# Turning and copying q and k of two early quads apart, in a squared-ReLU attention with a mixture of adapters, and a new order of work

## The chip, the cores and the metric

The kernel runs on one core of one Trainium2 chip. The core has a matrix engine (PE; PEld is its weight load), a vector engine (DVE), an activation engine (ACT), a general engine (POOL) and an engine for synchronisation and transfers (SP). The metric is the time of one execution in microseconds on the device. Median before: 184.39 us of 4 runs, from 184.19 to 185.39.

## The reference

Two stages follow each other. The first is attention without softmax: 8 batches, 12 heads, sequence 448, head dimension 64. The second takes the attention's output as 3584 rows of 768 and adds the output of two of eight low-rank adapters (rank 16) to each row, weighted by a gate.

```python
def _attn_ref(q, k, v):
    scores = 1.0 / np.sqrt(64) * np.matmul(q, k.transpose(0, 1, 3, 2))
    attn = np.maximum(scores, 0.0) ** 2 / 448
    return np.matmul(attn, v)

def _moe_ref(x, w_gate, A, B):           # x: the attention's output, (3584, 768)
    logits = x @ w_gate                  # 8 experts, the two largest are kept
    # w: softmax over the two kept logits
    # delta = sum over the two experts e of w[e] * (x @ A[e]) @ B[e]
    return x + delta
```

## The kernel before

**Tiling.** Four heads of one batch make a *quad*; there are 3 quads in each of 8 batches, 24 in all. A quad's 448 keys are cut into J = 7 blocks of 64, so the attention is 168 steps n, each a block of keys of one quad against all its 448 queries. Inputs come as float32 and are turned to bf16 by the load itself (`load`, L299: two DMAs of 64 partitions each, issued on POOL).

**A quad's way through the engines.**

- `tp` (L421): PE turns q and k so that the head dimension lies on the partitions. Each turn is 28 small matmuls with the identity (L431), 28 for q (`m`) and 28 for k (`m1`), both into one pair of PSUM banks: q in columns 0 to 447 of each bank, k in 448 to 895, as bf16. One DVE copy of 128x1792 (`ev`, L445) then brings both to the tile `qT`. With `tboth=1` the turns of q wait for the loads of q and of k.
- The first quad is treated apart (L456 to L481). Its k comes in two pieces: three blocks by SP and ACT (`raw`), four by POOL (`k_rest`, L339). The pieces are turned into bank pairs of their own and copied by `piece` (L448, profile line L453); the copy of the k rest is `e2`, 128x512.
- `qk` (L552, matmuls at L565) makes the scores of a step in two banks; at most three steps' scores are held at a time.
- `relu` (L576) scales and clips them to bf16, on ACT (L585) or on DVE (L587); `sq` (L595, L603) squares two or three steps at a time on DVE; `pv` (L610, L629) multiplies by v and sums over a quad's 7 steps.
- `xt_copy` (L647, L658) brings the attention's output to SBUF, turned, as `xt`.

**The second stage.** A table `awg` is made from A and the gate's weights: two loads (L368, L370) and a selector matrix made on POOL (L361, L362), then two fills of 36 pairs of matmuls (`aw_place`, L375; L383), each copied by DVE (L390). For groups of up to three tiles of 128 rows, `gate` multiplies `xt` by `awg` (L675), picks the two largest logits (L696 to L715), scales (`zp`, L719) and turns the result (L736, L745). `outputs` (L777) adds x and the product with B on PE (L790, L795), copies it out of PSUM (L825, L830) and stores it (L846).

**What sets the order.** The program is written out in an order that the kernel itself works out before it is built. `build` makes a list of operations, each with engines that may do it, a duration, the operations that it depends on, and a rank. `schedule` (L122) plays them through on a model: whenever an engine is free, the ready operation of the lowest rank goes (for PE a change of the tiling mode adds `switch`, and a score step goes ahead when ACT would otherwise run dry). Each engine then carries out its operations in that order, strictly, and waits where an input is not there. Three sets of numbers steer this. `C` holds offsets of rank for each kind of operation. `RANKS` adds a quarter of its value to the rank of single operations by their index in the list, and `ENGINES` fixes the engine of some. The landing time of a load comes from `Dma.land` (L111): half a load's time for each of its two DMAs, stretched by 1.3 while the model's DMA clock lies between 4.5 and 13 us, plus 1.5 us, or 2.1 once that clock is past 5. In the plan at most four loads are in flight ("lane").

Index 84 and 86 in the list are the two fills of `awg`, 85 is the copy of the first of them.

Of the kernel before, what the change touches and what calls it, by code (L numbers as in the profile page):

```python
# [14 lines left out]
J = 7  # L15
# [5 lines left out]
S = J * PH  # L21
# [12 lines left out]
def parts(*cuts):  # L34
# [3 lines left out]

C = dict(
    tp_=2.3287, qk_=-3.679, sq_=3.7975, pv_=3.3372, xt_=-1.2131, gate_=-0.65203, id_=-0.78412,  # L40
    out_=-0.80943, zt_=6.6019, a12=(4, 7), late=6, merge_x=0, id2=2.6063, ocap=3, tboth=1, sqs=(2, 2, 3), xback=(15, 23), xblat=1.4, xbdur=1.35, bx=8, xlag=6, xh=2, gl=(2, 1), tqk=-25.0, tqlat=2.0,
    slack=0.12096, switch=5.8257, third=10.0, dve_relu=0.24094, relu_until=400, qk=-2.3217, sq=10,
    pv=1.0506, xt=8.4423, tp=-9.2867, tpe=4.3867, gate_mm=-4.8593, gate=-1.4524, zt=0.2432, zte=2.902,
    id=15.183, out=3.032, pace=6.5353,
)
# [2 lines left out]


RANKS = {  # L50
    0: 9, 125: -15, 128: -31, 133: -17, 144: -3, 165: -18, 170: 51, 171: -5, 174: -25, 177: -13, 179: 16,
    181: -26, 184: -21, 204: 56, 205: 58, 209: 45, 219: -34, 221: 16, 222: 40, 224: -72, 226: -72, 229:
    31, 260: 33, 263: -15, 264: -19, 268: -26, 272: -6, 276: -17, 281: -15, 287: -22, 290: -135, 293:
    -132, 295: -52, 298: -1, 301: -8, 304: -45, 305: -13, 307: -44, 315: -1, 316: -1, 326: 29, 337: 47,
    340: 49, 342: -28, 345: -33, 347: -4, 374: -3, 375: -1, 380: -85, 396: 6, 403: -19, 424: 19, 430: 22,
    432: 12, 448: 88, 451: -48, 453: -40, 490: 2, 495: -21, 496: -4, 500: -13, 503: -15, 507: -16, 510:
    -39, 517: 1, 519: -27, 525: -62, 548: 5, 558: 40, 561: 96, 567: 48, 569: 5, 580: -56, 603: -3, 621:
    -65, 629: -58, 634: -19, 638: -43, 658: -3, 660: -34, 664: 65, 685: 36, 688: 19, 690: -49, 696: -8,
    697: 12, 701: -45, 713: 11, 722: 22, 779: -1, 780: 18, 790: 25, 794: -24, 795: 100, 799: 43, 801: 44,
    804: -68, 805: 13, 806: -37, 807: 86, 823: 5, 824: 23, 828: -53, 830: -65, 838: 10, 844: 7, 866: -83,  # L60
    867: 31, 870: 7, 871: -68, 874: -80, 878: -91, 896: -49, 898: -65, 916: -51, 920: -15, 923: -17, 924:
    -13, 925: -21, 933: 52, 950: 73, 966: 55, 982: -1, 991: -90, 1008: -109, 1021: 35, 1033: 45, 1043:
    -18, 1066: -10,
}
ENGINES = {
    107: "ACT", 109: "ACT", 170: "DVE", 199: "ACT", 215: "DVE", 222: "DVE", 291: "ACT", 373: "DVE", 381:
    "ACT", 402: "ACT", 431: "ACT", 447: "ACT", 457: "DVE", 517: "ACT", 568: "ACT", 573: "ACT", 581:
    "ACT", 677: "DVE", 866: "ACT", 903: "ACT", 981: "ACT", 1036: "ACT",
}

MODE_SWITCH = 0.13
# [11 lines left out]
def dve(n, rate=0.96):  # L83
    return n / (1000.0 * rate) + 0.068
# [20 lines left out]
class Dma:  # L105
# [5 lines left out]
    def land(self, t, o):  # L111
        if o.kind != "load":
            self.free = max(self.free, t - o.dur[o.engs[0]] + 0.6) + o.mb
            return max(self.free + 1.3, t + o.lat)
        if o.engs[0] != "POOL":
            return t + o.lat
        for x in (t - o.dur["POOL"] / 2, t):
            self.free = max(self.free, x + 0.5) + o.mb / 2 * (1.3 if 4.5 < self.free < 13 else 1)
        return self.free + (1.5 if self.free < 5 else 2.1)


def schedule(ops, c=C):  # L122
# [139 lines left out]
def build(k=None, c=C):  # L262


    ops, more, T = [], [], {}
    nc = k.nc if k else None

    def op(*a, to=ops, **kw):
        o = Op(*a, **kw)
        to.append(o)  # L270
        return o
# [18 lines left out]
    PE, DVE, ACT, ANY = ("PE",), ("DVE",), ("ACT",), ("ACT", "DVE")  # L290
# [119 lines left out]
    while n < NS:  # L410
        m = c["sqs"][turn % len(c["sqs"])]
# [7 lines left out]
    loaded, tp_ops, qk_ops, relu_ops, sq_ops, pv_ops, xt_ops = {}, {}, {}, {}, {}, {}, {}  # L419

    def tp(b, q):  # L421


        rank = first_use[b, q] + at("tp", first_use[b, q])
# [56 lines left out]
            return [[e1, *es] + [e2] * (j >= CUT) for j in range(J)]  # L481
        if b >= c["bx"]:
            return turn_qk(b, q)
        m = op(PE, 0.225, lambda: mm(m, 0), deps=[loaded[b, w, q] for w in range(1 + c.get("tboth", 0))], mode="64",
               kind="tp", ni=56, banks=("t", 2), take=("qT",), rank=rank)
        m1 = op(PE, 0.225, lambda: mm(m, 1), deps=[loaded[b, 1, q], m], after=m, mode="64", kind="tp", ni=56,
                give=("k", "q"), rank=rank - 0.5)
        if c.get("tsplit"):
            es = [op(ANY, {"ACT": act(2 * S), "DVE": dve(2 * S, 1.92)}, None, deps=[m1], free=[(m, g)], rank=rank + c["tpe"])
                  for g in range(2)]  # L490
            for g, e in enumerate(es):
                def fn(g=g, e=e):
                    if ("qT", b, q) not in T:
                        new("qT", ("qT", b, q), [128, 2, 2, S], BF16)
                    (nc.scalar.copy if e.eng == "ACT" else nc.vector.tensor_copy)(
                        T["qT", b, q].rearrange("p g w x -> p g (w x)")[:, g], k.ps_b[:, m.banks[g], : 2 * S])
                e.fn = fn
            return [es] * J
        e = op(DVE, dve(4 * S, 1.92), ev, deps=[m1], free=[(m, None)], rank=rank + c["tpe"])
        return [[e]] * J  # L500

# [526 lines left out]
```

## Time and profile before

| | us |
|---|---|
| median of 4 runs | 184.39 |
| the profiled execution | 184.01 |
| its span | 181.9 |
| PE, DVE, ACT, POOL busy | 165.4, 164.5, 155.1, 89.9 |
| granted PE clock, mean over the span | 0.977 |
| end of the last matmul; end of the last copy | 177.4; 178.0 |

The span runs from the first instruction to the last, and the last 3 us or so of it are the stores that land after the last copy. "Busy" counts the time in which an instruction of the engine is under way; neighbours on DVE and ACT can overlap by some tenths of a microsecond. In a row of the timeline, neighbours of one kind are merged: "x4" and a length of 3.35 us are four instructions that end 3.35 us after the first began, and the bracket tells the idle time of the engine before the first and who ended it. PEclk is the matrix engine's granted clock, in tenths of full speed.

### The profile page before, as it was taken

How to read it: one execution, taken by the hardware profiler on the slowest of the kernel's cores; microseconds unless marked ns; L12 is line 12 of the kernel's file. 1: busy time of each engine (PE TensorE's matmuls, PEld its weight loads, DVE VectorE, ACT ScalarE, POOL GpSimd, SP SyncE). 2: the span in 40 equal slices, each digit the busy share in tenths (PEclk: the TensorE clock that was granted, in tenths of full speed). 3: DMA queues.
4: the chain of work that ended last, by engine and by line, in shares of the span. 5: the costliest groups of instructions: out<-in, count | busy, mean ns of one | idle time of the engine just before them, and what ended most of it. 6: DMA issues, size and time to landing. Idle time of an engine off the chain costs nothing.

```text
span 181.9 us, 7406 instructions
## 1 busy us (share of the span) xinstructions
PE 165.4 (91%) x3198; PEld 97.1 (53%) x3198; DVE 164.5 (90%) x258; ACT 155.1 (85%) x226; POOL 89.9 (49%) x155
## 2 busy tenths in 40 slices
PE   7559987869999989999999899999999999999990
PEld 2435854635565556546556466565566456456650
DVE  1568999999999999999999999999999999999941
ACT  3479889999999999999999999999999999961210
POOL 7999789897975979755277636700000000000000
PEclk9956999999999999999999999999999999999998
DMA  5999999999999999999989999999873457555766
GB/s 92 129 159 149 191 188 178 178 169 191 162 199 208 224 227 188 225 193 217 190 129 178 213 223 126 199 134 174 101 123 70 108 130 164 140 140 126 220 178 172
DMA packets 34449, 30.49 MB, mean 168 GB/s; under 512 B 11952, under 2 KB 30896, under 8 KB 34416
## 3 DMA queue, kind: packets, MB, share of 16 engines
q0 software_dynamic: 22000, 17.03, 66.6%
q1 hardware_dynamic: 11792, 11.90, 27.3%
q10 hardware_dynamic: 624, 1.08, 2.3%
q8 instruction: 25, 0.41, 0.9%
q14 instruction: 8, 0.07, 0.2%
HBM read 33.84 MB, written 11.01 MB: 247 GB/s over the span
## 4 chain that ended last, share of the span: by engine, by line
PE 55%; DVE 26%; ACT 11%; issue 4%; DMA 2%; POOL 0%; DVEq 0%; ACTq 0%; POOLq 0%
PE ps L795 19%; PE ps L565 13%; DVE a L603 12%; PE ps L629 11%; ACT a L585 9%; DVE qT L445 6%; PE ps L675 4%; PE ps L790 4%; PE ps L431 3%; DVE xt L658 3%; DVE a L587 2%; DMA q<-in_q_dram 2%; ACT xt L658 1%; PE ps L736 1%; DVE zp L719 1%
## 5 line engine op out<-in xcount | busy, mean ns | idle before, releaser
L585 ACT ACTIVATE a<-ps 128x896 bf16<-128x896 f32 x157 | 136.4, 957 | 5.1 <-PE ps L565 4.8
L603 DVE TENSOR_TENSOR a<-a 128x1792 bf16<-128x1792 bf16 (+1 forms) x72 | 88.2, 1240 | 2.4 <-ACT a L585 2.2
L565 PE MATMUL ps<-qT 64*64 64x448 bf16 x672 | 62.0, 372 | 8.1 <-ACT a L585 4.1
L795 PE MATMUL ps<-B,zT 128*128 128x384 f32 x112 | 47.0, 514 | 0.0
L629 PE MATMUL ps<-a,v 64*64 64x448 bf16 x672 | 44.5, 351 | 1.5 <-DVE qT L445 1.1
L565 PEld LDWEIGHTS <-qT 64*64 64x64 bf16 x672 | 23.9, 107 | 38.0 <-issue 28.0
L307 POOL DMA_DIRECT2D q<-in_q_dram x48 | 29.4, 632 | 16.2 <-PE ps L431 8.5
L307 POOL DMA_DIRECT2D v<-in_v_dram x48 | 29.4, 636 | 6.9 <-PE ps L565 2.6
L307 POOL DMA_DIRECT2D k<-in_k_dram x46 | 28.2, 634 | 3.8 <-DMA q<-in_q_dram 3.1
L629 PEld LDWEIGHTS <-v 64*64 64x64 bf16 x672 | 22.4, 106 | 12.2 <-issue 5.1
L445 DVE COPY qT<-ps 128x1792 bf16<-128x1792 bf16 x23 | 25.0, 1086 | 0.7 <-PE ps L431 0.5
L795 PEld LDWEIGHTS ps<-B,zT 128*128 128x128 f32 x112 | 17.5, 191 | 4.8 <-issue 1.3
L658 ACT CAST xt<-ps 128x448 bf16<-128x448 f32 x25 | 13.9, 585 | 3.4 <-PE ps L629 3.4
L658 DVE CAST xt<-ps 128x448 bf16<-128x448 f32 x23 | 14.0, 617 | 0.3 <-PE ps L629 0.3
L830 ACT COPY osb<-ps 128x384 f32<-128x384 f32 x24 | 12.2, 530 | 1.4 <-PE ps L795 1.4
L587 DVE TENSOR_SCALAR a<-ps 128x896 bf16<-128x896 f32 x11 | 12.0, 1088 | 1.3 <-PE ps L565 1.0
L790 PEld LDWEIGHTS <-xt 128*128 128x128 bf16 x114 | 7.8, 97 | 9.3 <-issue 7.7
L790 PE MATMUL ps<-identb,xt 128*128 128x128 bf16 x114 | 12.7, 221 | 0.0
L431 PEld LDWEIGHTS <-q 64*64 64x64 bf16 x672 | 10.5, 115 | 4.0 <-issue 2.5
L675 PE MATMUL ps<-awg,xt 128*128 128x136 bf16 x168 | 12.5, 223 | 0.0
L675 PEld LDWEIGHTS <-xt 128*128 128x128 bf16 x168 | 10.1, 98 | 3.2 <-issue 3.0
L431 PE MATMUL ps<-identb,q 64*64 64x64 bf16 x672 | 10.5, 199 | 0.6 <-ACT a L585 0.5
(47 smaller groups left out, 96.8 us busy)
## 6 DMA issues: line engine op xcount, KB each, us to landing
out_dram<-osb SPq DMA_DIRECT2D x50, 192.0 KB, 3.5
q<-in_q_dram POOLq DMA_DIRECT2D x48, 112.0 KB, 4.5
v<-in_v_dram POOLq DMA_DIRECT2D x48, 112.0 KB, 5.1
k<-in_k_dram POOLq DMA_DIRECT2D x46, 112.0 KB, 4.9
out_dram<-osb ACTq DMA_DIRECT2D x4, 192.0 KB, 2.7
B<-in_moe_B_dram POOLq DMA_DIRECT2D x1, 384.0 KB, 5.0
xb<-xt SPq DMA_TRANSPOSE x18, 4.0
a_raw<-in_moe_A_dram POOLq DMA_DIRECT2D x1, 192.0 KB, 4.9
```

What stands on the lines that cost most here:

```text
L307: nc.gpsimd.dma_start(out=t[g * PH : g * PH + PH], in_=k.qkv[w][b, g, :, 2 * q : 2 * q + 2, :])
L431: nc.tensor.transpose(k.ps_b[sl * PH : sl * PH + PH, o.banks[g], (w * J + j) * PH : (w * J + j) * PH + PH], source(w, j)[r, sl], k.identb[ ...
L445: nc.vector.tensor_copy(t.rearrange("p g w x -> p g (w x)"), k.ps_b[:, m.banks[0] : m.banks[0] + 2, : 2 * S])
L565: nc.tensor.matmul(out=bank(o, sl)[g * PH : g * PH + PH, at : at + w], lhsT=t[r, g, 1, j * PH : j * PH + PH], rhs=t[r, g, 0, x0:x1], start ...
L585: nc.scalar.activation(out, flat(qk_ops[n], w), ACTF.Relu, scale=k.relu_scale)
L587: nc.vector.tensor_scalar(out, flat(qk_ops[n], w), k.relu_scale, 0.0, op0=ALU.mult, op1=ALU.max)
L603: nc.vector.tensor_mul(a2, T["a1", g0], T["a1", g0])
L629: nc.tensor.matmul(out=bank(head, g)[sl * PH : sl * PH + PH, :w], lhsT=vn[r, sl, j * PH : j * PH + PH], rhs=T["a2", g0][r, i, sl * w : sl ...
L658: evac(w, lambda cp, g=g: cp(k.xt[:, g * QUADS + q, b * S + x0 : b * S + x1], bank(src, g)[:, :w]), deps=[pv_ops[n]], free=[(src, g)], ran ...
L675: nc.tensor.matmul(out=bank(zops[0])[:, t * ZW : t * ZW + ZW], lhsT=k.xt[:, do, 128 * tiles[t] : 128 * tiles[t] + 128], rhs=k.awg[:, do, : ...
L790: nc.tensor.matmul(out=out(h)[:, x * 128 : x * 128 + 128], lhsT=k.xt[:, 3 * h + x, c0 : c0 + 128], rhs=k.identb, start=(x == 0), stop=Fals ...
L795: nc.tensor.matmul(out=out(h)[:, :W], lhsT=T["zT", g0][:, zi], rhs=k.B[:, h * W : h * W + W], start=xb is not None, stop=True, skip_group_ ...
```

## The change

The second and third quads (the quads with index 1 and 2, `apart=3`) no longer turn q only when k has landed too: `m` waits for q alone. A copy `eq` of q (128x896) follows `m`, and a copy `e` of k follows `m1` and `eq`. The score steps of these quads wait for both copies. The other 21 quads and the first are done as before. The bank pair is given back after `e`.

In `Dma.land` the stretch by 1.3 now ends at 8 us instead of 13, and the landing term stays at 1.5 up to 16 us instead of 5. Four planner constants, nearly all of `RANKS` and most of `ENGINES` are new; the arithmetic is the same.

```diff
-... sqs=(2, 2, 3), xback=(15, 23), xblat=1.4, xbdur=1.35, bx=8, xlag=6, xh=2, gl=(2, 1), tqk=-25.0, tqlat=2.0,
-    slack=0.12096, switch=5.8257, third=10.0, dve_relu=0.24094, relu_until=400, qk=-2.3217, sq=10,
+... sqs=(2, 2, 3), xback=(15, 23), xblat=1.4, xbdur=1.35, bx=8, xlag=6, xh=2, apart=3, gl=(2, 1), tqk=-25.0, tqlat=2.0,
+    slack=-0.19633, switch=5.8334, third=4.0894, dve_relu=0.28627, relu_until=400, qk=-2.3217, sq=10,
...
 RANKS = {
-    0: 9, 125: -15, 128: -31, 133: -17, 144: -3, 165: -18, 170: 51, 171: -5, 174: -25, 177: -13, 179: 16,
...
+    0: 5, 84: 115, 85: 162, 86: 87, 132: 10, 141: 53, 148: -11, 150: 39, 155: -32, 156: -8, 157: 13, 158:
+    -9, 160: -12, 163: -20, 166: -25, 170: -15, 179: -51, 185: -11, 191: -5, 192: 35, 200: 50, 210: 36,
...
 ENGINES = {
-    107: "ACT", 109: "ACT", 170: "DVE", 199: "ACT", 215: "DVE", 222: "DVE", 291: "ACT", 373: "DVE", 381:
-    "ACT", 402: "ACT", 431: "ACT", 447: "ACT", 457: "DVE", 517: "ACT", 568: "ACT", 573: "ACT", 581:
-    "ACT", 677: "DVE", 866: "ACT", 903: "ACT", 981: "ACT", 1036: "ACT",
+    140: "ACT", 178: "ACT", 233: "ACT", 265: "ACT", 286: "ACT", 298: "ACT", 568: "ACT", 634: "DVE", 852:
+    "ACT", 866: "ACT", 881: "ACT",
 }
...
-            self.free = max(self.free, x + 0.5) + o.mb / 2 * (1.3 if 4.5 < self.free < 13 else 1)
-        return self.free + (1.5 if self.free < 5 else 2.1)
+            self.free = max(self.free, x + 0.5) + o.mb / 2 * (1.3 if 4.5 < self.free < 8 else 1)
+        return self.free + (1.5 if self.free < 16 else 2.1)
...
-        m = op(PE, 0.225, lambda: mm(m, 0), deps=[loaded[b, w, q] for w in range(1 + c.get("tboth", 0))], mode="64",
+        apart = 3 * b + q < c["apart"]
+        m = op(PE, 0.225, lambda: mm(m, 0), deps=[loaded[b, w, q] for w in range(1 + (not apart))], mode="64",
                kind="tp", ni=56, banks=("t", 2), take=("qT",), rank=rank)
...
+        if apart:
+            eq = op(DVE, dve(2 * S, 1.92), lambda: piece(nc.vector.tensor_copy, m, 0, 0, J), deps=[m], rank=rank + c["tpe"] - 0.5,
+                    to=more)
+            e = op(DVE, dve(2 * S, 1.92), lambda: piece(nc.vector.tensor_copy, m, 1, 0, J), deps=[m1, eq],
+                   free=[(m, None)], rank=rank + c["tpe"])
+            return [[eq, e]] * J
```

## The prediction

> **What bounds the kernel now.** I read the page's busy shares and its 40 slices first (a slice is 4.55 us), then busy time by stretch, then the timeline where those rows show holes.
>
> ```profile
> span 181.9 us, 7406 instructions
> PE 165.4 (91%) x3198; PEld 97.1 (53%) x3198; DVE 164.5 (90%) x258; ACT 155.1 (85%) x226; POOL 89.9 (49%) x155
> PE   7559987869999989999999899999999999999990
> DVE  1568999999999999999999999999999999999941
> ACT  3479889999999999999999999999999999961210
> PEclk9956999999999999999999999999999999999998
> ```
>
> From the fifth slice to about 161 us ACT and DVE are nearly full; from 50 us PE is too. Only the two ends have slack: the last 16 us belong to PE alone (ACT is down to 2 tenths or less from 164 on), the first 24 to nobody. Busy time by stretch (start:end, length, then busy us and instructions in brackets):
>
> ```profile
> 10.50:14.20 3.70, 2.42 (x76) 1.42 (x72) 2.46 (x3) 3.31 (x5) 3.70 (x7) 0.50 1.06 153
> 20.50:24.00 3.50, 3.32 (x114) 2.47 (x112) 3.50 (x6) 2.49 (x4) 3.45 (x6) 1.00 1.09 228
> 24.00:30.00 6.00, 4.36 (x114) 2.48 (x114) 6.00 (x7) 6.00 (x9) 5.50 (x11) 1.00 1.18 175
> 140.00:161.00 21.00, 20.92 (x283) 10.72 (x275) 20.81 (x36) 20.09 (x30) 0.00 (x0) 1.00 0.56 130
> ```
>
> PE works 20.92 of 21.00 us before the tail, but only 4.36 of 6.00 between 24 and 30, where ACT and DVE are full. So work that starts earlier on ACT and DVE can be followed by PE; the end moves if the lead is kept. The timeline (start, length, what; in brackets the idle before it and who ended it) shows what is late:
>
> ```profile
> 7.14 1.09 DVE L587 TENSOR_SCALAR a<-ps 128x896 bf16<-128x896 f32 x1 [0.84 <-PE ps L565]
> 8.34 1.09 DVE L603 TENSOR_TENSOR a<-a 128x1792 bf16<-128x1792 bf16 x1
> 9.35 0.42 DVE L453 COPY qT<-ps 128x512 bf16<-128x512 bf16 x1
> 9.82 1.33 PE L565 MATMUL ps<-qT 64*64 64x448 bf16 x12 [2.40 <-DVE qT L453]
> 10.46 3.35 ACT L585 ACTIVATE a<-ps 128x896 bf16<-128x896 f32 x4 [1.78 <-PE ps L565]
> 11.41 1.09 DVE L603 TENSOR_TENSOR a<-a 128x1792 bf16<-128x1792 bf16 x1 [1.64 <-ACT a L585]
> 12.41 1.08 DVE L445 COPY qT<-ps 128x1792 bf16<-128x1792 bf16 x1
> 14.19 2.54 ACT L585 ACTIVATE a<-ps 128x896 bf16<-128x896 f32 x3 [0.39 <-PE ps L565]
> 21.01 1.73 ACT L585 ACTIVATE a<-ps 128x896 bf16<-128x896 f32 x2 [0.46 <-PE ps L565]
> 23.28 9.93 ACT L585 ACTIVATE a<-ps 128x896 bf16<-128x896 f32 x12 [0.55 <-PE ps L565]
> ```
>
> A copy of 0.42 us stands behind a square of 1.09 us; PE, then ACT, then DVE wait in turn. ACT loses 1.78 + 0.39 + 0.46 + 0.55 = 3.18 us before 24, and not a microsecond more until 50. DVE loses 1.64, and 0.34 and 0.29 later: 2.27.
>
> **The change, part by part.** The order is the planner's, so I ask what its new constants make it believe. By its load rule (issue ends 1.17 us apart on POOL, half a load's time each, plus a landing term), the rest of the first k lands at 7.43 by the old constants and 6.83 by the new; the trace has its second issue at 3.71 and 2.8 to landing: 6.5. The k of the second quad: 10.94, now 10.34; the trace: 6.06 + 3.9 = 9.95. The k of the third: 14.45, now 13.04; the trace: 8.43 + 4.4 = 12.85. All three come nearer.
>
> 1. The copy of 0.42. Its turns ended at 7.41. Believed ready at about 7.3, not 7.85, it stands right after the relu that ends at 8.23 and ahead of the square: done at 8.65 instead of 9.77. ACT took up the next relu 0.69 after the copy (10.46 − 9.77): now at 9.34. ACT's 1.78 shrinks to 9.34 − 8.68 = 0.66. Gain 1.12. The displaced square is late by 0.42, and only PV at 16.83 waits for that chain.
>
> 2. Second quad apart. The turns of q can go at 8.3, when q lands (4.91 + 3.4), and their copy before k lands at 9.95. Then k: some 0.7 of turns at half clock (10.57 to 11.28 for q in this trace), a half copy. No row has a 128x896 copy; between 0.39 for 448 columns and 1.09 for 1792 it is 0.39 + 448 x 0.70/1344 = 0.62. Copied by 11.4, or by 12.5 behind one square of 1.09; ACT could begin the second quad 0.7 later, at 12.1 to 13.2. ACT's own work is there at 9.34 + 3.35 = 12.69. Before it was 14.19: gain 1.0 to 1.5 with step 1 in it; I take 1.4. The third quad's k is there at 12.85, and ACT needs it seven relus (5.9 us) after 12.7: splitting it gains nothing. Two splits cost 2 x (2 x 0.62 − 1.09) = 0.30 on DVE; half of that, 0.15, is felt, as DVE and ACT share work.
>
> Here a rule speaks against the change. The Trainium skill, "PSUM — Partial Sum Buffer", section "PSUM bank collisions raise a hardware error", says two engines must be kept out of one bank and quadrant at the same time, whatever columns they touch. The split q and k share one pair of banks (the first quad's pieces have their own, so no row shows the wait). If the program obeys it, k's turns wait on PE for the q copy on DVE, and all of PE's later work stands behind them. By the columns alone step 2 costs no wait; by the rule it costs nothing if the q copy is done by 9.95, and up to a square, 1.09, if it is queued behind one. That leaves 0.3 of the 1.4 at worst. I take the rule as true and its cost as 0.1: q has 1.65 us ahead of k.
>
> 3. The gate table. Two fills of 36 small matmul pairs stand at 18.84 and 21.30 (1.5 to 1.7 us each); ACT's 0.46 and 0.55 follow them. Ranks +115/4 and +87/4 push both fills back, +162/4 one of their evictions (0.57 each). POOL is reordered too: four loads may be in flight in the plan, and earlier landings free a slot sooner. By hand, the first v passes the two POOL instructions for the selector (0.87 and 0.83), the table's two loads (13.00 to 14.45) fall behind later k, v and q loads to about 18.6. So k of the fourth quad is issued some 1.45 earlier (lands near 19.2, not 20.7), and the table lands at 18.6 + 4.9 = 23.5, not 17.9. SP has nothing here. Gain on ACT: up to 1.01; I take 0.8.
>
> Its price: 3.0 us of PE now lie after 24. PE's idle there is 1.64 up to 30 and 1.50 from 30 to 40, 3.14 together; but a fill in one piece of 1.5 against ACT's 0.87 per relu can starve ACT as it did at 21. I charge 0.8, between 0 (all in the holes) and 1.0 (the two stalls again).
>
> 4. DVE's idle of 2.27 is room for at most two relus (1.09 there, 0.87 off ACT). Between 0 and 1.74 I take 0.4, as the squares also come sooner.
>
> 5. The clock. The Trainium skill, "TensorE: Matmul & The Clock Gate", section "What's actually happening", has PE fall to half speed after an idle window of about 3.4 us. The trace fell with a shorter gap: 2.40 us, and 0.50 granted from 10.5 to 14.2; score matmuls average 517 ns from 4 to 16.8 us, 359 from 30 to 60. By the rule the smaller gap keeps the clock full and may save some 0.3 (an estimate, from 0.69 to about 0.4) at each of two hand-overs; by the trace sparse work keeps it low. ACT sets the pace, so I take 0.
>
> 6. Everything after. Most new ranks lie beyond 50 us, and half the forced engines go. No row shows that order. PE idles 2.15 us between 50 and 161, so at most 2.1 is to be had; were all 111 us as loose as 60 to 80 (0.97 idle in 20) the idle would be 5.4, a loss of 3.2. The nearest row is the present order: 0.
>
> Sum: 1.4 − 0.15 − 0.1 + 0.8 − 0.8 + 0.4 = 1.55, say 1.6. The profiled execution took 184.01 (span 181.9 and 2.1 around it): 182.4. The median, 184.39, lies 0.38 above: **182.8**. A measurement of this kernel can tell about 0.5% (0.92 us) from no change.
>
> **Rivals.** *Carried through* (above): full ACT and DVE from 24, and PE's holes there, speak for it. 0.55; own range 181.5 to 183.6.
>
> *Bank wait*: the split does not start k's turns freely; they wait behind a late q copy once or twice. 1.1 is given back: 183.9. For it: the 1.09 squares on the same engine. Against: q's lead of 1.65. 0.12.
>
> *Absorbed*: the lead turns into more PE idle between 24 and 50, or is lost in the new order, because PE sets the tail. Lead 1.6, minus as much: 184.4. Against it: in the present trace PE follows ACT there at three quarters load. 0.13.
>
> *Slower: the table comes too late.* The gate's first matmuls (L675) stand at 33.6 and the outputs (L795) begin at 46.5. With one eviction pushed by 40 ranks, the gate for the first tiles waits, PE has nothing to fill 34 to 50 with (idle 2.2 already), and the outputs go to the end, where PE is alone: 2.4 us of L795 before 50 and 1.2 of L675, 3.6 in all. 184.4 − 1.6 + 3.6 = 186.4. It decides once more than 2.5 us of them are displaced. For it: the ranks. Against: outputs are 12.8 us of the tail anyway, and the gate runs well before its outputs. 0.20, in which I include a plainly poorer order in step 6.
>
> **How the numbers follow.** Faster: 0.53 of the first, 0.05 of the bank wait, 0.02 of absorbed: 0.60. Same: the rest of those, 0.20. Slower: 0.20. The range takes the low end of the first (181.5) and the slower case up to 186.2, leaving under 0.08 below and 0.12 above.
>
> **What would show it.** Step 1: the 0.42 copy before the square, and ACT's hole at 8.7 under 0.8. Step 2: two half copies near 0.62, the second quad's relus from about 12.7; a PE wait on the q copy would show the bank rule. Step 3: fills after 23.5, no ACT holes near 20 to 23. Carry: at 50 us the same copy of qT about 1.6 earlier, and outputs after 161 still near 12.8 us. The prediction is wrong if PE's idle between 50 and 161 exceeds 2.15 by more than 1, or L795 begins after 50.

## The result, and the profile after

The changed kernel takes 183.75 us (median of 35 runs, 181.71 to 187.25), the kernel before, run beside it, 184.22 (54 runs, 183.36 to 185.39). The ratio of the two is **0.9956, with an interval of 0.9940 to 0.9971**: 0.44% or 0.8 us faster, against 1.6 us predicted. The ratio leaves out runs that are more than 1.5% above the fastest of the same kernel; the changed kernel's fastest run is exceptionally low, so this drops its upper part (8 of 35), and the medians over all runs give 183.75/184.22 = 0.9974. A second set of runs of the same kernel gave 0.998 (0.9958 to 1.0002), and over both sets together (57 runs and 100 beside them) the medians are 183.95 and 184.24. The gain lies between 0.3 and 0.8 us, at the edge of what can be told from no change. The profiled execution is that fastest run of the 35: 181.71 us (span 179.9). Its profile shows the change at its best, and what the other runs lose has to be looked for elsewhere.

The page of the changed kernel, busy shares and the rows of the 40 slices (4.5 us each):

```profile
span 179.9 us, 7410 instructions
PE 163.7 (91%) x3198; PEld 96.6 (54%) x3198; DVE 164.9 (92%) x257; ACT 155.3 (86%) x229; POOL 89.8 (50%) x155
PE   7867698897999999999999999999999999999990
DVE  1599999999999999999999999999999999998860
ACT  3599999999999999999999999999999999951200
PEclk9999999999999999999999999999999999999997
```

DVE and ACT are full from the third slice on, not from the fifth or sixth, and the clock row has lost its 5 and 6. Busy time by stretch of the changed kernel (start:end, length, then PE, PEld, DVE, ACT, POOL with instructions in brackets, granted clock, DMA share, GB/s):

```profile
10.50:14.20 3.70, 2.12 (x80) 1.46 (x81) 3.70 (x5) 3.70 (x6) 3.62 (x7) 1.00 1.06 155
20.50:24.00 3.50, 2.81 (x100) 1.84 (x100) 3.50 (x4) 3.50 (x6) 2.95 (x5) 1.00 1.48 223
24.00:30.00 6.00, 5.62 (x164) 4.21 (x156) 6.00 (x8) 5.95 (x9) 4.77 (x9) 1.00 1.19 195
50.00:161.00 111.00, 109.03 (x2098) 63.80 (x2091) 109.21 (x165) 108.89 (x163) 44.95 (x76) 1.00 0.89 170
140.00:161.00 21.00, 20.76 (x324) 11.40 (x324) 20.59 (x31) 19.45 (x28) 0.00 (x0) 1.00 0.49 113
```

From 10.5 to 24 neither DVE nor ACT idles. PE has 5.62 us of work between 24 and 30 where it had 4.36, because the two fills of the gate table now stand there. Between 50 and 161 PE idles 111.00 − 109.03 = 1.97 us, no more than before (2.15). The timeline of the changed kernel at the start (DVE and ACT rows in order of time):

```profile
7.16 14.85 ACT L591 ACTIVATE a<-ps 128x896 bf16<-128x896 f32 x18 [0.69 <-PE ps L571]
7.38 0.42 DVE L452 COPY qT<-ps 128x512 bf16<-128x512 bf16 x1 [1.08 <-PE ps L430]
7.76 1.09 DVE L593 TENSOR_SCALAR a<-ps 128x896 bf16<-128x896 f32 x1
9.14 0.62 DVE L452 COPY qT<-ps 128x896 bf16<-128x896 bf16 x1 [0.29 <-PE ps L430]
9.69 1.08 DVE L609 TENSOR_TENSOR a<-a 128x1792 bf16<-128x1792 bf16 x1
10.69 0.62 DVE L452 COPY qT<-ps 128x896 bf16<-128x896 bf16 x1
...
13.73 0.61 DVE L452 COPY qT<-ps 128x896 bf16<-128x896 bf16 x1
...
15.73 0.61 DVE L452 COPY qT<-ps 128x896 bf16<-128x896 bf16 x1
...
22.29 2.58 ACT L591 ACTIVATE a<-ps 128x896 bf16<-128x896 f32 x3
```

ACT runs 18 relus in one piece from 7.16 to 22. The copy of 0.42 us stands ahead of the square, ahead even of the first DVE relu, and the half copies of the second and third quad take 0.61 to 0.62. The table's loads are issued at 19.01 and 19.91 (before: 13.00 and 13.90), have landed at 25.2 (before: 18.1), and the fills start at 25.4 (before: 18.84). In the changed kernel:

```profile
19.01 0.91 POOL L367 DMA_DIRECT2D a_raw<-in_moe_A_dram  x1
```

and in the kernel before:

```profile
13.00 0.96 POOL L368 DMA_DIRECT2D a_raw<-in_moe_A_dram  x1
...
18.84 1.68 PEld L383 LDWEIGHTS <-sel 128*128 128x128 bf16 x36 [0.34 <-issue]
```

### Where the lead goes

For the changed kernel and those that keep its order after the start, I took the relus in order of their start, numbered from 0, seven to a quad, and subtracted their starts from those of the kernel before's profile. This "lead" is positive where the run is ahead. Number 21 opens the fourth quad, 63 the tenth, 84 the thirteenth; "last output" is the lead at the end of the last matmul. A load is two transfers, and its landing is that of the later one. The last column but one is a stop of PE that is explained below. *again* is the changed kernel unaltered; the others are described with the experiments.

| profiled execution | second quad's k landed | third quad's q landed | clock 11 to 22 us | lead at 21 | at 63 | at 84 | last output | PE stop near 68 us | span |
|---|---|---|---|---|---|---|---|---|---|
| before | 10.0 | 11.6 | 0.75 | 0 | 0 | 0 | 0 | none | 181.9 |
| after | 10.0 | 11.6 | 1.00 | 3.59 | 2.51 | 1.96 | 2.29 | none | 179.9 |
| again | 10.1 | 12.0 | 0.84 | 2.92 | 1.32 | −0.88 | −0.88 | 1.47 | 183.1 |
| pause | 10.6 | 12.0 | 1.00 | 3.34 | 2.26 | 0.21 | 0.54 | 1.32 | 181.7 |
| room | 10.4 | 12.7 | 0.84 | 3.31 | 2.28 | 0.70 | 0.91 | 0.85 | 181.3 |
| late_a | 12.1 | 12.7 | 0.84 | 1.43 | 0.35 | −0.74 | −0.70 | 0.36 | 182.9 |
| merged | 10.5 | 13.0 | 0.53 | 1.01 | 0.03 | −0.52 | −0.20 | none | 182.4 |

Three things can be read from it. The start lead is 1.0 to 3.6 us, and smallest in the two executions with the latest loads: the second quad's k in *late_a*, the third quad's q in *merged*. From 21 to 63 the order gives back the same 0.98 to 1.08 in five of the six (in *again* 1.60: it had one more stop, 0.48 us at 31.9), and from 63 to 84 another 0.55 where PE doesn't stop. Where PE stops, the loss from 63 to 84 is the 0.55 and the stop and some 0.18 more: 2.20 for 1.47, 2.05 for 1.32, 1.58 for 0.85, 1.09 for 0.36.

### The profile page after: what moved, and what is told of

It is laid out like the page before. It is cut to its first block, busy times and chain, and to the rows that moved or that the text cites. A ratio compares the mean times of both kernels' runs of the same rounds, so it can differ in the third digit from the quotient of the medians.

```text
span 179.9 us, 7410 instructions
## 1 busy us (share of the span) xinstructions
PE 163.7 (91%) x3198; PEld 96.6 (54%) x3198; DVE 164.9 (92%) x257; ACT 155.3 (86%) x229; POOL 89.8 (50%) x155
## 3 DMA queue, kind: packets, MB, share of 16 engines
q1 hardware_dynamic: 11792, 11.90, 25.2%
q10 hardware_dynamic: 624, 1.08, 2.3%
## 4 chain that ended last, share of the span: by engine, by line
PE 57%; ACT 17%; DVE 16%; issue 4%; DMA 2%; POOL 2%; ACTq 0%; DVEq 0%; POOLq 0%
PE ps L801 19%; ACT a L591 14%; PE ps L571 13%; PE ps L635 11%; DVE a L609 8%; PE ps L681 4%; PE ps L796 4%; PE ps L430 2%; DVE qT L444 2%; ACT xt L664 2%; DMA q<-in_q_dram 2%; DVE a L593 2%; PE ps L382 2%; DVE xt L664 2%; DVE qT L452 1%
## 5 line engine op out<-in xcount | busy, mean ns | idle before, releaser
L591 ACT ACTIVATE a<-ps 128x896 bf16<-128x896 f32 x155 | 133.6, 965 | 1.2 <-PE ps L571 0.9
L571 PE MATMUL ps<-qT 64*64 64x448 bf16 x672 | 57.7, 362 | 7.4 <-ACT a L591 5.6
L635 PE MATMUL ps<-a,v 64*64 64x448 bf16 x672 | 43.0, 350 | 1.7 <-ACT a L591 1.6
L571 PEld LDWEIGHTS <-qT 64*64 64x64 bf16 x672 | 22.7, 105 | 35.5 <-issue 27.6
L635 PEld LDWEIGHTS <-v 64*64 64x64 bf16 x672 | 21.7, 106 | 12.0 <-issue 4.6
L444 DVE COPY qT<-ps 128x1792 bf16<-128x1792 bf16 x21 | 22.8, 1084 | 0.1
L664 ACT CAST xt<-ps 128x448 bf16<-128x448 f32 x28 | 15.2, 576 | 3.6 <-PE ps L635 3.6
L593 DVE TENSOR_SCALAR a<-ps 128x896 bf16<-128x896 f32 x13 | 14.1, 1087 | 0.5 <-PE ps L571 0.4
L796 PE MATMUL ps<-identb,xt 128*128 128x128 bf16 x114 | 12.7, 221 | 0.2
L664 DVE CAST xt<-ps 128x448 bf16<-128x448 f32 x20 | 12.2, 618 | 0.7 <-PE ps L635 0.5
L681 PEld LDWEIGHTS <-xt 128*128 128x128 bf16 x168 | 10.4, 98 | 4.4 <-issue 3.9
L430 PEld LDWEIGHTS <-q 64*64 64x64 bf16 x672 | 10.5, 111 | 3.6 <-issue 0.9
L430 PE MATMUL ps<-identb,q 64*64 64x64 bf16 x672 | 10.4, 195 | 0.7 <-DMA q<-in_q_dram 0.3
```

The lines of the kernel that those rows point to most:

```text
L430: nc.tensor.transpose(k.ps_b[sl * PH : sl * PH + PH, o.banks[g], (w * J + j) * PH : (w * J + j) * PH + PH], source(w, j)[r, sl], k.identb[ ...
L444: nc.vector.tensor_copy(t.rearrange("p g w x -> p g (w x)"), k.ps_b[:, m.banks[0] : m.banks[0] + 2, : 2 * S])
L571: nc.tensor.matmul(out=bank(o, sl)[g * PH : g * PH + PH, at : at + w], lhsT=t[r, g, 1, j * PH : j * PH + PH], rhs=t[r, g, 0, x0:x1], start ...
L591: nc.scalar.activation(out, flat(qk_ops[n], w), ACTF.Relu, scale=k.relu_scale)
L593: nc.vector.tensor_scalar(out, flat(qk_ops[n], w), k.relu_scale, 0.0, op0=ALU.mult, op1=ALU.max)
L635: nc.tensor.matmul(out=bank(head, g)[sl * PH : sl * PH + PH, :w], lhsT=vn[r, sl, j * PH : j * PH + PH], rhs=T["a2", g0][r, i, sl * w : sl ...
```

## The experiments

Unless an edit says otherwise nothing of the computation is changed; each kernel is compared with the kernel before, run beside it.

| kernel | what it is | median, us | before | ratio |
|---|---|---|---|---|
| again | changed kernel, unaltered | 184.20 | 184.28 | 0.998 (0.9958 to 1.0002) |
| swap | before, copy of 0.42 ahead of the square | 184.37 | 184.28 | 1.0001 (0.9975 to 1.0028) |
| merged | after, one copy for q and k as before | 183.51 | 184.28 | 0.9951 (0.9927 to 0.9975) |
| latefill | before, three ranks of the table as after | 195.08 | 184.28 | 1.0535 (1.0484 to 1.0586) |
| warm1 | after, 4 zero matmuls at each early score step | 184.61 | 184.23 | 1.0019 (0.9993 to 1.0046) |
| warm2 | after, 8 zero matmuls at fewer steps | 184.49 | 184.23 | 1.0016 (0.9995 to 1.0037) |
| warmb | before, 4 zero matmuls | 188.02 | 184.23 | 1.0201 (1.0164 to 1.0238) |
| swap2 | swap, and the table issued earlier | 183.54 | 184.23 | 0.9966 (0.9943 to 0.9988) |
| late_a | after, second quad's q and all later loads issued some 0.7 later | 184.77 | 184.15 | 1.0017 (0.9996 to 1.0038) |
| late_b | before, second quad's q and all later loads issued some 0.7 later | 184.96 | 184.15 | 1.0049 (1.0029 to 1.0069) |
| room | after, q turned later, third quad in one copy | 183.68 | 184.15 | 0.9969 (0.9942 to 0.9995) |
| pause | after, POOL pauses 3.2 us | 184.35 | 184.25 | 1.0001 (0.9978 to 1.0025) |

### The parts of the start: again, swap, merged, latefill

*again* repeats the changed kernel, to learn how much of the profiled 2.3 us an ordinary execution shows.

> The changed kernel once more, unaltered, for a second profile and the spread of its times. Its first profile (181.71) is the fastest of its 35 executions; their median is 183.75. Theory A, the clock: the executions near 183.5 have lost 1.5 to 2 us in the first 25 us to a PE at half clock; then a profile with a time of 183 or more shows a granted clock near 0.5 somewhere between 8 and 20 us and holes of ACT there of 1 us or more, and over the executions time falls as the mean clock rises. Theory B, loads: PE or DVE wait 1 us or more for a landing at a clock that stays full. Theory C, the middle: the start is as in the first profile, with the fourth quad's first relu near 22.3, and the 2 us go after 50 us.

It measured 0.998, and its profile lies at 184.9, 1.2 us of span longer than before. The same program's two profiled executions differ by 3.2 us; one profile of this order doesn't stand for its median.

*swap* does step 1 alone, in the order of the kernel before:

```diff
+    ops = schedule(build(h))
+    tags = [getattr(o, "tag", None) for o in ops]
+    i, j = tags.index(("sq", 0)), tags.index("rest")
+    ops.insert(j, ops.pop(i))
```

> The kernel before, with one change: in the finished order the copy of the rest of k stands ahead of the first square on DVE instead of behind it. All else keeps its place. Carried through: the copy ends 1.1 us earlier, ACT takes up its fourth relu at about 9.3 instead of 10.5, and the end comes 0.6 to 1.1 us earlier: ratio to the kernel before 0.994 to 0.997. Rival, the order of the rest decides: a start that is 1.1 us earlier is waited away by 50 us, ratio 1.000 within 0.002.

The time is unchanged. The lead is 1.58 at relu 7 and 1.19 at relu 14, and −0.91 at relu 21. Timeline of *swap*: PE's wait, what ACT pays for it, and POOL's issue of the table:

```profile
13.91 0.96 POOL L368 DMA_DIRECT2D a_raw<-in_moe_A_dram  x1
...
20.12 0.22 PE L383 MATMUL ps<-a_raw,sel 128*128 128x128 bf16 x1 [2.39 <-DMA a_raw<-in_moe_A_dram]
...
22.11 1.73 ACT L586 ACTIVATE a<-ps 128x896 bf16<-128x896 f32 x2 [2.76 <-PE ps L566]
```

PE arrives at the first fill, whose place is fixed, 2.39 us before the table has landed; in the kernel before PE got there at 18.84 and the table was there at 18.1, 0.7 us ahead. Step 1 gains what was said, and the next thing late is the table. Of the 2.39, about 0.9 is that execution's own: it issued the table that much later than the kernel before's profile did (13.91 against 13.00).

*merged* keeps the changed order and leaves out the split: the first half copy is gone, and the second copies q and k together.

```diff
-            eq = op(DVE, ..., lambda: piece(nc.vector.tensor_copy, m, 0, 0, J), deps=[m], ...
+            eq = op(DVE, ..., lambda: None, deps=[m], ...
-            e = op(DVE, ..., lambda: piece(nc.vector.tensor_copy, m, 1, 0, J), deps=[m1, eq],
+            e = op(DVE, ..., ev, deps=[m1, eq],
```

> The changed kernel with q and k of the second and third quads copied in one instruction at the place of the second of the two copies; q's own copy is gone, everything else keeps its place. If the split itself brings something: the one copy of 1.09 ends some 0.45 us later than the half copy did, ACT waits for it once, and the time is 0.2 to 0.5 us above the changed kernel's. Rival, the split is worth nothing: ACT has relus to do until then, DVE gets 0.15 us back for each quad, and the time is the changed kernel's within 0.2.

It is as fast as the changed kernel: 0.9951 against 0.9956 and 0.998. What the split brings or costs is below what these runs can tell; the gain is that of the order. Its profile had late loads (the third quad's q at 13.0, against 11.6) and a cold matrix engine, as its busy time by stretch shows:

```profile
11.00:22.00 11.00, 9.34 (x188) 5.44 (x189) 8.98 (x9) 9.38 (x12) 10.72 (x19) 0.53 1.14 162
```

The same stretch of the changed kernel:

```profile
11.00:22.00 11.00, 7.50 (x204) 3.87 (x205) 11.00 (x12) 11.00 (x15) 10.60 (x18) 1.00 1.11 161
```

PE needs 9.34 us at the clock of 0.53 and 7.50 at 1.00, and ACT loses 1.6.

*latefill* moves the table's fills alone: the three ranks of the changed kernel in the kernel before.

```diff
-    0: 9, 125: -15, ...
+    0: 9, 84: 115, 85: 162, 86: 87, 125: -15, ...
```

> The kernel before with three ranks of the changed one: the two fills of the gate table 115/4 and 87/4 later, the copy of the first 162/4 later. The planner plays the order through again, so the rest can move too. Carried through: ACT's two holes of 0.46 and 0.55 near 20.5 and 23 are gone, its relus after 24 are 0.8 to 1.0 earlier, and the end comes 0.3 to 0.8 earlier (ratio 0.996 to 0.998). Rival, the table comes too late: the gate starts later than 33.6, PE has more idle time before 50, and the time is the same or up to 1.5 us longer.

5.4% slower. Waits of *latefill* from 20 to 161 us (engine, line, releaser: us in total, times, longest):

```profile
ACT a L585 <- PE ps L565: 10.1, 16, 1.9
```

ACT is starved 16 times, from 21 to 48 us and again near the end; the lead is −3.4 at relu 42 and −11.1 at 140. The edit did not do what it was meant to: the planner laid out the whole program anew from the three ranks, with all the others still tuned to the old order. It says nothing on step 3, but it does say that searched ranks can't be carried over one by one. All later edits therefore move single operations in the finished order.

### The clock: warm1, warm2, warmb

The half clock of *merged* suggested that the gain is lost where PE runs cold between 10 and 22 us. These kernels put matmuls of zeros into the early score steps, into the bank that the step is about to overwrite, so the result is unaffected.

```diff
+            for sl in range(2 if 3 <= n <= 20 else 0):
...
+                for g in range(2):
+                    nc.tensor.matmul(out=bank(o, sl)[g * PH : g * PH + PH, at : at + w],
+                                     lhsT=k.zeros[r, :PH], rhs=k.zeros[r, :w], start=True, stop=True)
```

> The changed kernel with four more matmuls of zeros ahead of each score step 3 to 20, into the banks that the step then overwrites; they wait for the banks alone, not for q and k, and fill PE's holes between 8 and 22 us. Theory A, the clock: in most executions PE falls to half clock there, and the lead at the fourth quad's first relu shrinks from 3.6 to 1 to 3 us; kept at work PE stays at full clock, the mean granted clock is 0.99 or more in most executions, and the median falls to 182.0 to 183.0 (ratio 0.988 to 0.993). Rival: the clock is a companion, not a cause; the median stays within 0.4 of 183.75, or rises by up to 1 us as the zeros delay the scores.

> As the run with four zeros a step, with eight a step on steps 3 to 16. If activity keeps the clock and four are too few, this one shows the clock at 0.99 or more and the gain of 0.8 to 1.7 us; if the zeros stand in the way of scores, it is 0.3 to 1.5 us slower than with four.

> The kernel before with the same four zeros a step on steps 3 to 20. Its hole of 2.4 us on PE at 7.4 stays, as the bank is the only thing the zeros need. Theory A: its scores of the first quads come at full clock, two hand-overs of some 0.3 us are saved, but its table fill holds the rest back as it waits for the table's landing near 18: 0 to 0.6 us faster. If it gains as much as the changed kernel does (0.8 or more), a warm PE is worth the same to any order and the change's own gain is not limited by it.

All three are slower than what they were made from, the two first by some 0.4 to 0.6%, the kernel before by 2%. Busy time by stretch of *warm2*:

```profile
11.00:22.00 11.00, 9.92 (x302) 6.20 (x290) 9.24 (x11) 9.39 (x12) 10.87 (x18) 1.00 1.13 164
```

and the waits of PE in *warm1* from 30 to 161 us (in its slowest execution, 187.53):

```profile
PE ps L430 <- issue: 3.7, 3, 2.2
```

The clock was full, and no time came of it: with the zeros PE's work in the stretch is 9.92 us, more than *merged* had at half clock, and ACT is no busier (9.39). In *warm1* PE stopped three times besides, 3.7 us together, for nothing that the profile shows ("issue"; taken up below). So the theory that the clock takes the gain isn't supported, but not refuted either: the zeros cost as much PE time as the full clock saves. The sign that was named for it, that time falls as the mean clock rises, did appear in *again*: 183.6 us in the median of the 8 executions with a clock of 0.99 or more, 184.8 in that of the 4 below 0.98. But late loads and a low clock can come together (*late_a* and *merged* in the table), so this doesn't make the clock the cause; and *warm2* had 0.99 or more in 18 of 22 executions and stayed at 184.5.

### Landing times: swap2, late_a, late_b

*swap2* is *swap* with the two table loads issued ahead of the fourth quad's q (one operation moved; the copy and square as in *swap*):

```diff
+    i, j = tags.index("table"), tags.index(("load", 1, 0, 0))
+    ops.insert(j, ops.pop(i))
```

> The kernel before with the copy of the rest of k ahead of the first square, and besides with the table's two loads issued before the fourth quad's q instead of after it. With the copy moved alone, PE waited 2.4 us at the first fill for the table's landing at 20.0 and the lead of 1.6 us was gone. If that wait is the whole reason: the table lands near 18, the wait is under 0.6, and the end comes 0.8 to 1.5 us earlier (ratio 0.992 to 0.996). Rival: the lead is lost in the rest of the order anyway, ratio 0.998 to 1.002.

0.9966, so 0.34% faster than before (0.12% to 0.57%). The table landed at 16.9 and PE no longer waits for it. The profiled execution lost its lead another way, before the table's place, so the evidence is the median. The timeline of *swap2* (POOL's issue, and ACT's hole for the third quad's late loads):

```profile
11.84 0.94 POOL L369 DMA_DIRECT2D a_raw<-in_moe_A_dram  x1
...
19.10 1.88 ACT L587 ACTIVATE a<-ps 128x896 bf16<-128x896 f32 x2 [1.76 <-PE ps L567]
```

Two moved operations give most of what the searched order gives. With *swap* this speaks for it that **the table must leave the way before the first copy is worth anything**, be it earlier or later. The two intervals just overlap, so the times alone don't show it; the wait in *swap* shows the place.

*late_a* and *late_b* delay the second quad's q and k, and with them all later loads, by a fill of zeros on POOL ahead of the load (0.77 us in the profile of *late_a*; the issue comes 0.67 to 0.68 later), in the changed kernel and in the kernel before. The tile that it fills isn't in use yet.

```diff
+            nc.gpsimd.memset(k.sel, 0.0)
```

> The changed kernel with one more fill of the selector on POOL (0.87 us) between the load of k's rest and the load of the second quad's q, so every later load, the table's too, is issued 0.87 us later. Theory B, landings: PE turns the second q at 8.6, and the third at 11.6, as soon as they land, and all of PE stands behind a turn that waits; the shift passes through, 0.5 to 0.9 us slower than the changed kernel (184.2 to 184.7). Rival, loads are no limit: the order has room, 0 to 0.2 slower.

> The kernel before with the same 0.87 us on POOL at the same place. Theory B: its turns stand behind its late copy and waited 0.2 us on loads in all; the second k lands at 10.8 where PE would turn it at 10.9, the third at 13.7 where it is turned at 15, the table at 18.8 where it is used at 18.8: 0 to 0.4 us slower, less than half of what the changed kernel loses. Rival: any order loses the same.

Both lose: the changed kernel goes from 0.9956 or 0.998 to 1.0017, the kernel before to 1.0049, about 0.7 to 1.1 us and 0.9 us. Late loads from the second quad on cost either order about their lateness. My theory that the new order stands tighter on its landings falls: if so, *late_a* would have lost clearly more than *late_b*.

### PE without instructions: room and pause

The stops "for nothing that the profile shows" are also in *again*. Its timeline:

```profile
68.64 0.29 PE L681 MATMUL ps<-awg,xt 128*128 128x136 bf16 x2
...
70.40 0.41 PE L681 MATMUL ps<-awg,xt 128*128 128x136 bf16 x4 [1.47 <-issue]
...
71.18 1.73 ACT L591 ACTIVATE a<-ps 128x896 bf16<-128x896 f32 x2 [1.42 <-PE ps L571]
...
72.13 1.09 DVE L609 TENSOR_TENSOR a<-a 128x1792 bf16<-128x1792 bf16 x1 [1.58 <-ACT a L591]
```

In the middle of one series of gate matmuls, with all operands there, PE does nothing for 1.47 us, and then ACT and DVE wait in turn. Counting PE's weight loads and matmuls from the start of the program, and three other instructions of PE's sequencer among them, every such stop of 0.36 us or more in the fourteen profiles (eleven: two in *again*, three in *warm1*, two in *warmb*, one each in *room*, *late_a*, *late_b*, *pause*) falls on an instruction whose number is 193 more than a multiple of 256; in *again*, *room*, *late_a* and *pause* it is number 2753. The queues of the changed kernel have one row that fits:

```profile
q8 instruction: 25, 0.41, 0.9%
```

25 transfers for 0.41 MB are 16.4 KB each; PE's 6396 weight loads and matmuls (and a few of its other instructions) at 25 blocks make 256 to a block. The DMA view of *again* in the stretch from PE's passing of instruction 2497 to the transfer's start, 63.4 to 67.9 us, has these queues:

```profile
q0 software_dynamic: 757, 0.60, 94.4%
q1 hardware_dynamic: 138, 0.35, 21.5%
```

and from 67.9 to 69.9 these (a transfer's whole time is counted where it begins, so that a share can pass 100%):

```profile
q0 software_dynamic: 434, 0.35, 109.8%
q1 hardware_dynamic: 36, 0.07, 11.4%
q8 instruction: 1, 0.02, 3.0%
```

In the changed kernel's profile, which didn't stop, the transfer falls between 64.4 and 66:

```profile
q0 software_dynamic: 186, 0.15, 65.0%
q1 hardware_dynamic: 92, 0.23, 40.3%
q8 instruction: 1, 0.02, 5.3%
```

Set against PE's passing of number 2497, the transfer that began next started this much later, and PE stopped at 2753 for so long:

| execution | transfer starts later by, us | stop, us |
|---|---|---|
| after | 2.21 | none |
| merged | 2.70 | none |
| late_a | 3.53 | 0.36 |
| room | 4.08 | 0.85 |
| pause | 4.38 | 1.32 |
| again | 4.52 | 1.47 |

PE needs 5.24 us for these 256 instructions. In the four that stop, the stop is the delay less 3.0 to 3.2, and PE goes on 2.2 to 2.4 us after the transfer began. The other boundaries agree: of 337 in the fourteen profiles, none is passed sooner than 2.18 us after the transfer for the next block began, and at all eleven stops PE goes on 1.3 to 1.6 us after that transfer ended. The stops also move with the count: *warm2*, with 224 instructions more in the same order, has its boundaries elsewhere and no stop, and loses the 0.55 alone between relus 63 and 84; *warm1*, with 144 more, has its stops in the turns of q and k. This shows that **PE stops because its instructions come late**. While q, k and v are loaded, the delays at the other blocks are 0.4 to 3.7 us, and the block at 2497 has the longest or nearly the longest of all in the four that stop. After the last load has landed (119 to 122 us) they are within 0.9 of nothing, but for single blocks at 1.3 and 1.5. A block of 6 or 7 us hides 3.7; this one, 5.24 us long, doesn't hide 3.5.

*room* asked whether less hurry at the start helps: the second quad's q is turned one score step later, the third's right before its k, and the third quad is copied in one piece.

```diff
+    place(("q", 0, 1), ("s", 4), 1)
+    place(("eq", 0, 1), ("q", 0, 1), 1)
+    place(("q", 0, 2), ("k", 0, 2))
```

> The changed kernel with room for late landings: on PE the second quad's q is turned one score step later than planned, the third quad's q directly ahead of its k, and the third quad is copied in one instruction. All else keeps its place. Theory B: PE's waits for q are gone in most executions, and the median falls 0.3 to 0.8 below the changed kernel's (183.0 to 183.4). Rival: the early turns cost nothing, the median stays within 0.2 of it or rises by up to 0.5 because the second quad's scores come later.

0.9969 (0.9942 to 0.9995): no different from the changed kernel. Start lead 3.31, and 0.85 lost again at instruction 2753.

*pause* was to keep the loads away from that transfer, by a break on POOL before one load (the selector's tile is filled with zeros, which nobody reads any more):

```diff
+            if (w, b, q) == (2, 4, 1):
+                for _ in range(4):
+                    nc.gpsimd.memset(k.sel, 0.0)
```

> The changed kernel with a break of about 3.5 us on POOL (four fills of the selector tile with zeros, which nobody reads by then) before the load of v of the fifth batch's second quad, which POOL issues at about 58 us; that load and the later ones are used some 20 us after they land. Nothing of the computation changes. Theory that PE's instructions are supplied late because their transfer stands behind the loads: in three of the five profiles that have this part of the order unchanged, PE's queue ran empty at its instruction 2753 (0.36, 0.85 and 1.47 us), and in all five the transfer of those instructions began 2.2 to 4.5 us after PE had passed instruction 2497. With no load under way at 62 to 64 us it begins within 1.5 us, PE does not stop at instruction 2753, and the median is 0.2 to 0.7 us lower than the changed kernel's: 0.991 to 0.996 of the time before. Rival, the transfer is late for another reason: it begins 2.2 to 4.5 us after as before, the stop is seen again in some executions, and the time is the changed kernel's, 0.995 to 0.998. Rival, the stop hardly matters to the median because it falls in few executions: the transfer is early but the time is 0.995 to 0.998. Slower than the kernel before (over 1.001) would mean that [...]the later loads come too late.

**The break missed its place.** I had counted the load two too early. Timeline of *pause*:

```profile
67.79 3.17 POOL L307 MEMSET sel<- 128x773 bf16 x4
```

and its waits from 20 to 161 us:

```profile
PE ps L684 <- issue: 1.3, 1, 1.3
```

It stands at 67.8, not at 58, so nothing differs when PE passes instruction 2497 at 62.5: the transfer came 4.38 us later and PE stopped 1.32, a sixth case for the table but no test of the cause. The time is 1.0001; the lead from relu 84 on is kept as in the changed kernel (0.21, then 0.54 at the end), so its profile shows no price of the break after the stop; why its median stands above the changed kernel's is open. That the transfer is late *because it stands behind the loads* remains argued, from the delays that go when the loads have ended and from q0's 94% to 110%. It wasn't tried.

## Why the prediction was right and where it was not

The time lies in the range (181.5 to 186.2) and 0.95 above the predicted 182.8; the ratio, 0.44% faster, is just inside the band that the text called no change, to which it gave 0.20, against 0.60 for more. The direction and the mechanism held, the size didn't.

**Step 1, the copy ahead of the square (1.12).** Right, and larger: *swap* had a lead of 1.58 at relu 7. That the square would not be missed was right too.

**Step 2, the second quad apart (0.28 on top, less 0.15 and 0.1).** The half copy worked out at 0.62 measured 0.61 to 0.62, and the second quad's relus began at 11.96 where 12.1 to 13.2 was said. But *merged* is as fast without the split: neither its gain nor its cost shows. The wait that the rule on PSUM banks led to expect is there. In the changed kernel k's turns come at 9.94, after the q copy (9.14 to 9.76), but in *again*, *pause* and *room* they start 0.06 us after that copy ends and are released by it, though `build` names no such dependence. Timeline of *again*:

```profile
9.56 0.62 DVE L452 COPY qT<-ps 128x896 bf16<-128x896 bf16 x1 [1.14 <-PE ps L430]
...
10.24 0.41 PE L430 MATMUL ps<-identb,k 64*64 64x64 bf16 x28 [0.23 <-DVE qT L452]
...
14.39 0.62 DVE L452 COPY qT<-ps 128x896 bf16<-128x896 bf16 x1 [0.44 <-PE ps L430]
```

k had landed at 10.07, so the wait cost 0.17 at most; in *pause* and *room* the later half of k landed only after it. The 0.1 was well weighed. In the third quad the order has k's turns (13.71 to 14.35) ahead of the q copy, and the last row shows that copy waiting for them: there the split brings nothing. Whether the program keeps the two engines apart for the bank or for the tile, the traces don't tell.

**Step 3, the table (0.8, price 0.8).** The places were right: landed at 25.1 (23.5 was estimated), fills at 25.4, no hole of ACT from 20 to 24. Its worth was put too low, in a way the working could have seen: "where a stall goes, say what is late next". With step 1 gained, PE reaches the fixed fill earlier than the table lands, and without step 3 the whole lead is lost there (*swap*). So the steps do not add: 1.12 without the table is 0. The price, 0.8, measured 0.98 to 1.08 from relu 21 to 63 in five executions; that it comes of the deferred fills (3 us of PE) is argued, not shown apart.

**Step 4 and 5, idle DVE (0.4) and the clock (0).** Together with 1 to 3 they make a start lead of 2.35 (without the price). Measured: 3.59, 2.92 and 3.34 in the three executions whose start has exactly this order, mean 3.28. The start brought more than said, not less. Zero for the clock can't be judged: *merged* shows cold hand-overs that cost ACT 1.6 us together with late loads, and the zeros could not separate the two.

**Step 6, everything after (0).** This is the step that failed. The bounds taken (2.1 to be had, 3.2 to be lost) hold, and the present order was taken as the nearest row. The new one gives back another 0.55 between relus 63 and 84, and regains 0.33 later; above all it sets a dense row of gate matmuls against a block of PE's instructions that comes late. The four profiles of the kernel before's PE order (*before*, *swap*, *swap2*, *late_b*) have one stop of that size in all, 0.96; the six of the new order have four at one place, 0.67 in the mean over six, and *again* one more. No row of the profile before showed such a wait, so no row could be the nearest to it. With measured terms, 3.28 − 1.08 − 0.55 + 0.33 = 1.98 is what the order gives where PE doesn't stop, a little more than the 1.55 of the sum; the stops of these three executions, (0 + 1.95 + 1.32)/3 = 1.09 and 0.18 beside each, take more than half of it, and the mean of their last outputs' leads is (2.29 − 0.88 + 0.54)/3 = 0.65. The medians say 0.5 and, for the repeat, 0.1; the ratios 0.8 and 0.4. Few executions were profiled, so this closes the account no better than to half a microsecond.

**The rivals.** *Bank wait* occurred in three of the profiles, at 0.17 us or less instead of 1.1. *Absorbed* gave the right size for another reason: PE's idle from 50 to 161 did not grow in the profile shown (1.97), but by the stops it is 3.40 in *again* and 3.28 in *pause*, over the mark of 3.15 that was set as a sign of being wrong. *Table too late* fell: the gate starts at 38.6 instead of 33.6, but the outputs at 46.40 (before 46.51), and after 161 us 10.8 us of them are left, 2.0 less than before.

## What to carry to other kernels

When a stall at the start is removed, follow the next engine to the first instruction at a fixed place that waits for a load: a lead is only worth the slack of what stands there, so the two have to be moved together, and two moved operations can do most of what a whole search does. Profile more than one execution before explaining a gain of a per cent: the two of this program that were profiled differ by 3.2 us, and only a comparison of leads at several points over several executions showed which part is the order and which the execution. Edit the finished order, not the ranks that a search tuned to each other.

## What the runs showed of the hardware that was not expected

PE's instructions arrive by DMA in blocks of 256 (16 KB), and PE can run out of them: 0.36 to 3.47 us at block boundaries in eleven stops, the longest in *warmb*'s slowest execution. The Trainium skill, "Runtime: NRT & Kernel Launch", section "Instruction fetch mechanics", states blocks of 16 KiB and 256 instructions, which these runs agree with, and calls the cost of a boundary "mostly hidden"; here it is hidden only if the block being run lasts longer than the transfer's delay and some 2.2 us, and the measurement decides. The profile lists such a stop as "issue" on PE, as it does every wait that it can't put down to something; one of over 0.3 us in the midst of a series of alike matmuls is worth counting off.

Loads issued at the same moments land at different times. The later half of the third quad's q, issued between 7.17 and 7.22 us in twelve profiles, landed between 11.6 and 13.6; in the three whose start has exactly the same order (*after*, *pause*, *again*) it landed at 11.6, 12.0 and 12.0, the second quad's q at 8.6, 9.1 and 9.0, and the leads after it are 3.59, 3.34 and 2.92.

The granted clock of these traces changes only at steps of 3.41 us, and the change goes with the time that matmuls were under way in the step. In the fourteen profiles, up to 172 us, a step at full clock with less than 1.9 us of them was always followed by one at half clock, one with more than 2.02 never. The kernel before had 1.07 us in the step from 6.34 to 9.76, *merged* 1.39, *again* 1.49 and *room* 1.81 in the steps that end near 11.5, and all four fell to half; the changed kernel had 2.62 in its step from 7.23 to 10.64 and stayed full. So a gap much shorter than a step (2.40 us before) is enough where the rest of the step is sparse.
